# One matmul in each unit and step of the seven-product stages streams 16 to 128 more columns

## The chip, the cores and the metric

The kernel runs on one core of a Trainium2 chip. The metric is the device time in microseconds (us); the time before is the median of three runs.

## What is computed

Causal block attention over 64 heads (8 batches of 8), 576 positions and 64 dimensions, followed by a feed-forward of 4608 tokens, 512 to 2048 to 512 wide, with a leaky ReLU between:

```python
mask = block_i >= block_j                       # blocks of 64 positions
scores = np.where(mask, scale * q @ k.T, -1e9)
attn = softmax(scores)
x = (attn @ v).transpose(0, 2, 1, 3).reshape(4608, 512)
h = x @ w_in
out = np.maximum(0.01 * h, h) @ w_out
```

## The kernel before

**Two parts.** The 4608 tokens are 18 chunks of 256 (`CH`). The first ten are computed with plain products while attention goes on: `ffn1` (L909, matmuls of 256 columns at L921) and `ffn2` (L940, matmuls of 512 columns at L948). The last eight chunks are the tail. It multiplies 2 by 2 blocks with seven products in place of eight, and it is these two seven-product stages that the change touches. Every operand is kept as a high and a low part, so that one product of 256 by 256 blocks is six matmuls: for each of two 128-row halves high by high and high by low, and low by high.

**First stage, `first8`.** It runs over `k` (four pairs of token chunks) and `u` (eight units): 32 units of seven products of six matmuls (L1160), all of 256 columns. Product `j` writes the first 256 columns of a bank of PSUM; five banks of the eight are taken in turn by each unit, and the second half of such a bank is not used. The stationary operand is a weight block or a sum of weight blocks (`stationary`), the moving one a block or sum of tokens (`operand`): `new` for `j` 0 to 2. VectorE adds the products together (`sum_of`, L1173), ScalarE applies the leaky ReLU (L1176), and DMAs store the result in DRAM (`gd`, L1205).

**Second stage, `second8`.** 32 steps `n`. Step `n` loads the token side back from `gd` (L1248), forms four sums (`op2`, L970 on VectorE and L971 on GpSimd), splits everything into high and low parts (a cast, L310 on ScalarE, then a subtraction at L970: the tiles `big` and `new`), and runs seven products of six matmuls (L1288), again of 256 columns. Steps are ordered by `k`, `s` and `q`; for `q` 0 to 3 the products add up in four banks. Three of these hold two products; the fourth (`spots[4 * s + 3]`) holds product 2 in its first half and nothing in its second. After `q` 3 VectorE combines the banks (L1311) and two DMAs store them (L1324).

**The order of the instructions.** Everything is handed as operations with choices of engine, estimated costs, a rank and dependencies to `Plan.add`. `Plan.run` (L151) plays these against estimated durations: at each moment an engine that is free takes the ready operation of lowest rank, and an operation that several engines could do goes to the one that is free first. The instructions are then issued in the order so found, each engine working through its own in order. The estimate for a matmul is `RATE` (0.4462 ns) for each column, that is 114.2 ns for 256 columns; `multiply` (L189) puts matmuls one behind the other with it. A changed estimate can therefore change which engine does what, and in which order, from that moment of the plan on; whatever the plan decided before that moment stays.

Of the kernel before, what the change touches and what calls it, by code (L numbers as in the profile page):

```python
# [17 lines left out]
P = 128  # L18
# [6 lines left out]
CH = 256  # L25
# [35 lines left out]
BY1 = None  # L61
RT8 = -1.36
RM = -38.787
PACE8 = 7
GATE8 = 5
RF8 = 8.016
# [28 lines left out]
RATE = 0.4462  # L95
# [17 lines left out]
class Plan:  # L113
# [19 lines left out]
    def add(self, choices, rank, reads=(), writes=(), lag=None, kind=None):  # L133
        i = len(self.ops)
        deps = set()
        for k in reads:
            if k in self.writer:
                deps.add(self.writer[k])
        for k in writes:
            if k in self.writer:  # L140
                deps.add(self.writer[k])
            deps.update(self.readers.get(k, ()))
        for k in reads:
            self.readers.setdefault(k, []).append(i)
        for k in writes:
            self.writer[k] = i
            self.readers[k] = []
        deps.discard(i)
        self.ops.append((choices, rank, deps, lag, kind))
# [127 lines left out]
def dve2(n):  # L277
    return n / 0.96 + 110
# [15 lines left out]
def attention_ffn(ctx: ExitStack, tc: tile.TileContext, q2: bass.AP, k2: bass.AP, qk: bass.AP, v: bass.AP, w_in: bass.AP, w_out: bass.AP, out: bass.AP):  # L294
    nc = tc.nc
# [10 lines left out]
    add = plan.add  # L306
# [35 lines left out]
    later = {}  # L342
# [47 lines left out]
    wide = ExitStack()  # L390
# [466 lines left out]
    def bank(b):  # L857
        if b == 0 and SPREAD:
            banks[1] += 1
            x = banks[1] % 4  # L860
            return x, (("t", x) if x < 2 else ("o", x - 2)), (p_t + p_o)[x]
        banks[0] += 1
        x = banks[0] % 2
        return x, ("t", x), p_t[x]
# [139 lines left out]
    def tail():  # L1004
        flat = lambda ap: ap.rearrange("p a b -> p (a b)")
        spots = [(("one", y), lambda y=y: later["single"][y]) for y in range(4)]
# [12 lines left out]
        new = x8s + [(key, u, y) for key in "ST" for u in range(NU) for y in range(2)]  # L1019
# [20 lines left out]
        def sum8(u, low, name="sum8"):  # L1040
            return later[name][u][:, low].rearrange("p a b -> p (a b)")
# [75 lines left out]
        def stationary(j, u, low, d):  # L1117
            if j in (0, 4):
                return sides(u, low)[:, d + (2 if j else 0)]
            if j in (2, 5):  # L1120
                return sides(u + NU, low)[:, d + (2 if j == 5 else 0)]
            return sum8(u, low)[:, ({1: 0, 6: 1, 3: 2}[j] * 2 + d) * P :][:, :P]
# [19 lines left out]
        def first8(k, u, rank):  # L1142
            five = [(count["bank"] + y) % 8 for y in range(5)]
            count["bank"] += 5
            halves = pairs[8 * k + u]
            uses = {0: 0, 1: 1, 2: 2, 3: 3, 4: 0, 5: 4, 6: 3}
            w0, w1, ws = wkeys[("wi", u)], wkeys[("wi", u + NU)], [("S", u, 0), ("S", u, 1)]
            weights = [w0, ws, w1, ws, w0, w1, ws]
            heap = lambda h, s: heaps[halves[h]]().rearrange("p (t s c) -> p t s c", t=2, s=2)[:, :, s]
            hk = [[hkey(halves[h])] for h in range(2)]  # L1150
            if k == 0 and u < 2:
                hk = [x + [["g"], ["ob"], [], [], []][halves[h]] for h, x in enumerate(hk)]

            def product(j):
                key, bank = spots[five[uses[j]]]
                terms = [(d, w, 0) for d in range(2) for w in range(2)] + [(d, 0, 1) for d in range(2)]

                def go(n):
                    d, w, x = terms[n]
                    nc.tensor.matmul(  # L1160
                        bank()[:, :CH], stationary(j, u, w, d), operand(j, x)[:, d],
                        start=j not in (4, 6) and n == 0, stop=n == 5, skip_group_check=j in (4, 6),
                    )

                add(
                    [("PE", [(RATE * CH, lambda n=n: go(n)) for n in range(6)])], rank + j / 10,
                    [("X", j, 0), ("X", j, 1)] + weights[j], [key],
                )
                return key, lambda: bank()[:, :CH].rearrange("p (t c) -> p t c", t=2)

            def sum_of(dst, one, two, plus, reads, writes, j):
                name = "tensor_add" if plus else "tensor_sub"
                add([("DVE", dve2(CH), lambda: getattr(nc.vector, name)(dst(), one(), two()))], rank + RG8 + j / 10, reads, writes)  # L1173

            def leaky(n, dst, src, reads, writes, j):
                add([("ACT", act(n), lambda: nc.scalar.activation(dst(), src(), AF.Prelu, alpha=0.01))], rank + RG8 + j / 10, reads, writes)  # L1176

            def store(h, src, dst, reads):
                add([("SP", ISSUE, lambda: nc.sync.dma_start(dst(), src()))], rank + RG8 + 0.8, reads, [("gd", k, u, h)], lag="gs")

            q, x = divmod(u, 2)
            k0, b0 = product(0)
            add(copying(CH, lambda: heap(0, 0), b0, sb=False)[:1], rank + RG8, [k0], hk[0])
            k1, b1 = product(1)
            sum_of(lambda: heap(0, 1), lambda: heap(0, 0), b1, True, [k1], hk[0], 1)
            k2, b2 = product(2)
            sum_of(lambda: heap(1, 0), lambda: heap(0, 1), b2, True, hk[0] + [k2], hk[1], 2)
            k3, b3 = product(3)
            sum_of(lambda: heap(1, 1), lambda: heap(1, 0), b3, True, [k3], hk[1], 3)
            product(4)  # L1190
            leaky(CH, lambda: heap(0, 0), b0, [k0], hk[0], 4)
            k5, b5 = product(5)
            sum_of(lambda: heap(1, 0), lambda: heap(1, 0), b5, False, [k5], hk[1], 5)
            leaky(2 * CH, heaps[halves[1]], heaps[halves[1]], [], hk[1], 5)
            product(6)
            sum_of(lambda: heap(0, 1), lambda: heap(0, 1), b3, True, [k3], hk[0], 6)
            leaky(CH, lambda: heap(0, 1), lambda: heap(0, 1), [], hk[0], 6)
            plan.writer["unit", 8 * k + u] = len(plan.ops) - 1

            def store(a, e, src, reads, by="SP"):  # L1200
                to = lambda: gd[k][q][:, a:e, :, x].rearrange("p b s c -> p (b s) c")
                queue = {"SP": nc.sync, "ACT": nc.scalar}[by]
                cost, late = (ISSUE, 0.8) if by == "SP" else (QUEUE, 0.6)
                add(
                    [(by, cost, lambda: queue.dma_start(to(), src().rearrange("p (x c) -> p x c", c=P)))], rank + RG8 + late,  # L1205
                    reads, [("gd", k, u, a)], lag="gs",
                )

            store(2, 4, heaps[halves[1]], hk[1])
            store(0, 2, heaps[halves[0]], hk[0], "ACT")  # L1210
# [11 lines left out]
        def second8(n, rank):  # L1222
            k, s, q = (0, n % 2, n // 2) if n < 8 else (n // 8, n // 4 % 2, n % 4)
            y, us = n % 2, (2 * q, 2 * q + 1)
# [46 lines left out]
            def operand(j, low):  # L1271
                part = 0 if j in groups[0] else 1
                return area(part, low)[:, groups[part].index(j) * CH :][:, :CH], part
# [7 lines left out]
            def product(j):  # L1281
                key, to = at(j)
                terms = [(x, 0, w) for x in range(2) for w in range(2)] + [(x, 1, 0) for x in range(2)]
                part = 0 if j in groups[0] else 1

                def go(m):
                    x, low, w = terms[m]
                    nc.tensor.matmul(  # L1288
                        to(), operand(j, low)[0][:, x * P : (x + 1) * P], moving(j, us[x], w),
                        start=q == 0 and m == 0 and j in opens, stop=q == 3 and m == 5 and (spot[j][1] == 1 or j == 2),  # L1290
                    )

                reads = [("Y", part, 0, y), ("Y", part, 1, y)]
                for u in us:
                    reads += wkeys[("wo", u)] if j in (0, 3) else wkeys[("wo", u + NU)] if j in (4, 6) else [("T", u, 0), ("T", u, 1)]
                add([("PE", [(RATE * CH, lambda m=m: go(m)) for m in range(6)])], rank + order.index(j) / 10, reads, [key])

            order = (4, 5, 6, 0, 1, 2, 3) if q == 0 else (0, 4, 1, 3, 2, 5, 6) if q == 3 else range(7)
            opens = [next(j for j in order if spot[j][0] == y) for y in range(4)]
# [13 lines left out]
            key, src = at(0)  # L1313
# [47 lines left out]
    order = sorted(range(NP), key=lambda c: begin[c])  # L1361
# [4 lines left out]
    for i in range(NH + 1):  # L1366
        if i == H:
            add([("POOL", 1, narrow)], 0, [], [("h", y) for y in range(2)])
        if i == PLAIN:
            new = [(key, y) for key in ("qh", "ql", "kh", "kl") for y in range(2)]  # L1370
            add([("POOL", 1, second_stage)], 0, [y for k in wkeys.values() for y in k], new)
            new = [x for y in range(TURNS) for x in turned_keys(y) + [("back", y, c) for c in range(6)]]
# [7 lines left out]
        for c in starts.get(i, ()):  # L1380
            for u in range(NU):
                rank = begin[c] + rate[c] * u / NU
# [43 lines left out]
```

## Time and profile before

| | |
|---|---|
| runs before | 1025.39, 1032.65, 1034.58 us (median 1032.65) |
| profiled execution | 1032.74 us, its span 1031.0 us |
| TensorE matmul busy | 1005.4 us of the span, 7432 matmuls |
| first seven-product stage | about 708.8 to 865 us of the span |
| second seven-product stage | about 865 to 1026.8 us |

Times in the rows are counted from the start of the span. A matmul's recorded duration includes a modelled end that overlaps the next one, so what a matmul costs in a row of many is read from the distance between starts.

### The profile page before, as it was taken

How to read it: one execution, taken by the hardware profiler on the slowest of the kernel's cores; microseconds unless marked ns; L12 is line 12 of the kernel's file. 1: busy time of each engine (PE TensorE's matmuls, PEld its weight loads, DVE VectorE, ACT ScalarE, POOL GpSimd, SP SyncE). 2: the span in 40 equal slices, each digit the busy share in tenths (PEclk: the TensorE clock that was granted, in tenths of full speed). 3: DMA queues.
4: the chain of work that ended last, by engine and by line, in shares of the span. 5: the costliest groups of instructions: out<-in, count | busy, mean ns of one | idle time of the engine just before them, and what ended most of it. 6: DMA issues, size and time to landing. Idle time of an engine off the chain costs nothing. (4 is left out here: it accounts for less than half of the span.)

```text
span 1031.0 us, 21866 instructions
## 1 busy us (share of the span) xinstructions
PE 1005.4 (98%) x7432; PEld 899.3 (87%) x7432; DVE 783.4 (76%) x1967; ACT 638.2 (62%) x1509; POOL 425.2 (41%) x418
## 2 busy tenths in 40 slices
PE   7889999999999999999999999999999999999998
PEld 4657889888888888888888888889999999999998
DVE  6898977777978788788887778707666676877775
ACT  6788768677767667777667677636445454434332
POOL 3334437554555445454665465512131141143331
PEclk9999999999999999999999999999999999999999
DMA  6545534686777777777787687664654658455442
GB/s 208 170 153 183 157 106 148 215 245 208 212 247 224 238 226 234 226 227 243 233 245 220 207 234 219 205 196 153 195 158 130 195 171 248 149 181 179 153 158 83
DMA packets 143103, 200.52 MB, mean 194 GB/s; under 512 B 15504, under 2 KB 113552, under 8 KB 142992
## 3 DMA queue, kind: packets, MB, share of 16 engines
q1 hardware_dynamic: 126096, 190.73, 59.8%
q10 hardware_dynamic: 16896, 8.39, 2.7%
q8 instruction: 59, 0.97, 0.4%
q14 instruction: 52, 0.43, 0.1%
HBM read 117.11 MB, written 81.95 MB: 193 GB/s over the span
## 5 line engine op out<-in xcount | busy, mean ns | idle before, releaser
L921 PE MATMUL p_h<-big,wih 128*128 128x256 f32 x1024 | 203.1, 279 | 0.4 <-ACT big L310 0.4
L948 PE MATMUL p_o<-woh,big 128*128 128x512 f32 x640 | 191.5, 394 | 0.7 <-ACT piles L310 0.7
L921 PEld LDWEIGHTS p_h<-big,wih 128*128 128x128 f32 x1024 | 165.2, 188 | 5.7 <-issue 1.0
L821 DVE STREAM_TRANSPOSE turn<-prow 128x128 f32<-128x128 f32 (+3 forms) x400 | 141.9, 396 | 10.2 <-ACT prow L658 5.2
L325 POOL TENSOR_TENSOR ks<-qk_in,ks 64x576 fp32r<-64x576 f32 x83 | 122.5, 1476 | 55.1 <-DVE p_v L610 27.2
L948 PEld LDWEIGHTS p_o<-woh,big 128*128 128x128 f32 x640 | 113.3, 188 | 20.8 <-issue 1.3
L325 POOL TENSOR_TENSOR big<-piles,big 128x512 fp32r<-128x512 f32 x64 | 85.8, 1340 | 107.3 <-ACT big L310 83.3
L921 PE MATMUL p_h<-big,wil 128*128 128x256 f32 x384 | 104.4, 277 | 0.0
L948 PE MATMUL p_o<-wol,big 128*128 128x512 f32 x320 | 99.5, 392 | 0.0
L626 ACT ACTIVATE prow<-p_s,nmrec 128x448 f32<-128x448 f32 (+4 forms) x150 | 83.0, 560 | 11.3 <-DVE nmrec L617 9.5
L656 POOL TENSOR_SCALAR prow<-prow,nmrec 128x192 f32<-128x192 f32 (+4 forms) x94 | 61.0, 655 | 69.9 <-DVE nmrec L643 36.3
L658 ACT ACTIVATE prow<-prow,nmrec 128x320 f32<-128x320 f32 (+4 forms) x154 | 81.8, 566 | 4.2 <-DVE nmrec L643 3.7
L736 PE MATMUL p_v<-turn,vt 128*64 128x256 f32 (+3 forms) x700 | 76.5, 367 | 1.6 <-ACT prow L626 1.4
L626 ACT ACTIVATE prow<-p_v,nmrec 128x576 f32<-128x576 f32 (+1 forms) x150 | 71.2, 483 | 10.2 <-DVE nmrec L617 9.4
L736 PEld LDWEIGHTS p_v<-turn,vt 128*64 128x64 f32 x700 | 47.0, 137 | 29.5 <-issue 15.2
L617 DVE TENSOR_REDUCE nmrec<-p_s 128x1 f32<-128x448 f32 (+4 forms) x150 | 71.8, 514 | 0.9
L921 PEld LDWEIGHTS p_h<-big,wil 128*128 128x128 f32 x384 | 72.1, 188 | 0.2
L948 PEld LDWEIGHTS p_o<-wol,big 128*128 128x128 f32 x320 | 60.1, 188 | 13.1
L936 ACT ACTIVATE piles<-p_h 128x512 f32<-128x512 f32 x80 | 47.4, 593 | 37.2 <-PE p_h L921 34.5
L921 PE MATMUL p_h<-xh,wih 128*128 128x256 f32 x256 | 69.7, 278 | 0.0
L921 PE MATMUL p_h<-xh,wil 128*128 128x256 f32 x256 | 69.7, 278 | 0.0
L971 POOL TENSOR_TENSOR x<-x 128x256 f32<-128x256 f32 x34 | 30.5, 901 | 76.3 <-DMA x<-gd 39.0
(244 smaller groups left out, 2576.4 us busy)
## 6 DMA issues: line engine op xcount, KB each, us to landing
way<-turn SPq DMA_DIRECT2D x50, 448.0 KB, 3.4
way<-turn SPq DMA_DIRECT2D x100, 168.0 KB, 3.4
turn<-way SPq DMA_DIRECT2D x100, 168.0 KB, 3.2
qk_in<-in_qk SPq DMA_DIRECT2D x50, 288.0 KB, 3.7
turn<-way SPq DMA_DIRECT2D x100, 112.0 KB, 3.0
out<-piles SPq DMA_DIRECT2D x36, 256.0 KB, 2.4
raw<-in_w_in SPq DMA_DIRECT2D x16, 512.0 KB, 3.8
raw<-in_w_out SPq DMA_DIRECT2D x16, 512.0 KB, 3.7
```

The source lines that it names most:

```text
L325: ("POOL", pool2(n), lambda: nc.gpsimd.tensor_sub(dst(), one(), two())),
L617: [("DVE", dve(kw[t]), lambda t=t, ap=ap, flat=flat: nc.vector.tensor_reduce(nm[z][: qn[t], at_col[t] : at_col[t] + 1], ap[: qn[t]], axis= ...
L626: nc.scalar.activation(o, ap[: qn[t]], AF.Exp, bias=nm[z][: qn[t], at_col[t] : at_col[t] + 1], scale=1.0, accum_out=sums[z][: qn[t], at_co ...
L656: ("POOL", pool1(kw[t]), lambda: nc.gpsimd.tensor_scalar(p(), p(), by, 1.0, op0=ALU.mult, op1=ALU.mult)),
L658: ("ACT", act(kw[t], True) + 108, lambda: nc.scalar.mul(p(), p(), by)),
L736: nc.tensor.matmul(dst, later["vt"][z][:, j], src, start=start, stop=stop)
L821: nc.vector.transpose(dst, src.rearrange("p (s b i) -> p s b i", b=4, i=32))
L921: nc.tensor.matmul(p_h[z][:, i, :], w[:, d, f * P : (f + 1) * P], (xl if x else xh[y])[:, d, :], start=first and k == 0 and (u > 0 or i == ...
L936: add([("ACT", act(512), lambda: nc.scalar.activation(g, p_h[z], AF.Prelu, alpha=0.01))], rank, [("h", z)], ["g"])
L948: nc.tensor.matmul(p_o[m], a[:, i, m * P : (m + 1) * P], w[:, u + NU * i, :], start=u == 0 and k == 0, stop=u == NU - 1 and k == 5,)
L971: ("POOL", pool2(n), lambda: getattr(nc.gpsimd, name)(dst(), one(), two())),
```

## The change

In each unit of `first8`, the first of the six matmuls of product 1 streams `CH + more` columns in place of `CH`, from the same stationary operand; `more` is 16, 32, 64 or 128 by `u % 4`. In each step of `second8` the same is done to the first of the six matmuls of product 2, with `more` by `k % 4`, where `k` is 0 for steps 0 to 7 and `n // 8` after that. The results of the extra columns land behind the 256 columns of the product, in a part of the bank that nothing reads. The estimate that the plan is given for these matmuls grows with the columns.

```diff
+MORE = [16, 32, 64, 128]
...
                 def go(n):
                     d, w, x = terms[n]
+                    if n == 0 and j == 1:
+                        wide = later["new"][:, 1].rearrange("p d c -> p (d c)")[:, : CH + more]
+                        nc.tensor.matmul(bank()[:, : CH + more], stationary(j, u, w, d), wide, start=True, stop=False)
+                        return
...
+                more = MORE[u % len(MORE)]
                 add(
-                    [("PE", [(RATE * CH, lambda n=n: go(n)) for n in range(6)])], rank + j / 10,
+                    [("PE", [(RATE * (CH + (more if n == 0 and j == 1 else 0)), lambda n=n: go(n)) for n in range(6)])], rank + j / 10,
...
                 def go(m):
                     x, low, w = terms[m]
+                    if m == 0 and j == 2:
+                        key, bank = spots[4 * s + 3]
+                        wide = sum8(us[0], 0, "tum8")[:, : CH + more]
+                        nc.tensor.matmul(bank()[:, : CH + more], operand(j, 0)[0][:, :P], wide, start=q == 0, stop=False)
+                        return
...
-                add([("PE", [(RATE * CH, lambda m=m: go(m)) for m in range(6)])], rank + order.index(j) / 10, reads, [key])
+                more = MORE[k % len(MORE)]
+                add([("PE", [(RATE * (CH + (more if m == 0 and j == 2 else 0)), lambda m=m: go(m)) for m in range(6)])], rank + order.index(j) / 10, reads, [key])
```

## Rows read from the trace of the kernel before

**Rows 1.** The page's busy times (share of the span) of each engine.

```profile
PE 1005.4 (98%) x7432; PEld 899.3 (87%) x7432; DVE 783.4 (76%) x1967; ACT 638.2 (62%) x1509; POOL 425.2 (41%) x418
```

**Rows 2.** Busy time by stage: us, busy of each engine, granted TensorE clock, DMA.

```profile
core 0: us, PE busy (x) PEld busy (x) DVE busy (x) ACT busy (x) POOL busy (x), PEclk, DMA share, GB/s
...
708.00:865.00 157.00, 156.58 (x1360) 155.33 (x1359) 106.66 (x237) 77.47 (x173) 35.73 (x33) 1.00 0.56 169
865.00:889.00 24.00, 21.72 (x176) 20.81 (x177) 17.62 (x26) 10.37 (x13) 4.37 (x5) 1.00 0.58 182
889.00:1027.00 138.00, 137.78 (x1170) 137.57 (x1169) 102.01 (x168) 51.48 (x62) 44.06 (x47) 1.00 0.46 151
```

**Rows 3.** Waits of PE, 708 to 1031 us: us in total, times, longest.

```profile
PE p_x L1288 <- DVE big L970: 1.7, 3, 0.8
PE p_h L1288 <- DVE big L970: 0.5, 1, 0.5
PE p_h L1160 <- ACT more L310: 0.3, 1, 0.3
PE p_x L1160 <- DVE xin L1173: 0.2, 1, 0.2
```

**Rows 4.** Chain that ended last, in order of time: start us, us, what.

```profile
860.92 1.36 PE p_h L1160 x12
...
866.69 6.39 DMA x<-gd
...
873.24 0.75 POOL x L971
...
874.92 1.06 ACT big L310
...
876.01 1.50 DVE big L970
...
881.99 3.92 DMA xin<-gd
...
887.19 1.23 DVE big L970
888.42 0.04 issue
888.47 4.75 PE p_x L1288 x38
...
908.06 19.79 PE p_x L1288 x168
...
1024.66 2.13 PE p_o L1288 x18
```

**Rows 5.** PE in order of time: start us, us, instruction, count; 512 columns, then 256.

```profile
703.26 0.62 PE L948 MATMUL p_o<-woh,big 128*128 128x512 f32 x2
...
708.76 0.28 PE L1160 MATMUL p_x<-new,wih 128*128 128x256 f32 x1
...
715.61 0.28 PE L1160 MATMUL p_x<-new,wih 128*128 128x256 f32 x1
...
721.73 0.28 PE L1160 MATMUL p_h<-new,wih 128*128 128x256 f32 x1
```

**Rows 6.** PE in order of time, attention's scores of 448 and 320 columns.

```profile
600.37 1.03 PE L596 MATMUL p_v<-ks,qs 128*128 128x288 f32 x7
601.23 0.86 PE L596 MATMUL p_s<-ks,qs 128*128 128x448 f32 x4
601.93 0.63 PE L948 MATMUL p_o<-woh,big 128*128 128x512 f32 x2
```

**Rows 7.** Groups by shape, 708 to 1031 us: busy us, mean ns, idle before.

```profile
L970 DVE TENSOR_TENSOR big<-xin,big 128x1024 fp32r<-128x1024 f32 x16 | 21.1, 1318 | 8.2 <-ACT big L310 8.1
L971 POOL TENSOR_TENSOR sum<-sum 128x768 fp32r<-128x768 f32 x4 | 7.9, 1976 | 26.1 <-ACT sum L310 26.1
```

## The prediction

> **What bounds the kernel now.** I read the busy times first, then the busy times by stage, then what TensorE waits for, and last the chain that ended last, each answering what the one before left open. TensorE has matmuls on record for 1005.4 of 1031.0 us, far ahead of VectorE's 783.4 [rows 1]. By stage: in the first seven-product stage it is busy for 156.58 of 157 us, around the change to the second for 21.72 of 24, and from 889 to 1027 for 137.78 of 138 [rows 2]. So in the stretch that the change touches TensorE has no room to take in more work. What it waits for there adds up to 1.7 + 0.5 + 0.3 + 0.2 = 2.7 us [rows 3]; 2.2 of them are waits for the low parts of `big` (L970 on VectorE) at the start of the second stage. The chain says the same: from 888.47 us to the end of the last product it is TensorE and nothing else (888.47 to 1024.66 + 2.13 = 1026.79), and ahead of that it runs for some 22 us through loads from `gd`, GpSimd, ScalarE and VectorE [rows 4]. The reader should see two regimes: 157 us and 138 us where a nanosecond added to TensorE is a nanosecond added to the end, and 24 us between them where the way through DRAM counts as well.
>
> **The change, part by part.**
>
> *The columns.* In `first8` each of the four values of `more` falls to 2 units in each of 4 pairs, 8 units in all: 8 x (16 + 32 + 64 + 128) = 1920 columns. In `second8` steps 0 to 7 have 16, and the next three eights 32, 64 and 128: again 1920. That is 3840 columns in 64 matmuls; no matmul, weight load, DMA, or instruction on another engine is added, and none is taken away.
>
> *The price of a column.* No row shows a matmul of 272 to 384 columns inside these stages, so I take it from distances between starts. The 24 matmuls of 512 columns from 703.26 to 708.76 us take 5.50 / 24 = 229.2 ns each; the 54 of 256 columns from 715.61 to 721.73 take 6.12 / 54 = 113.3 ns each [rows 5]. The slope between them is (229.2 - 113.3) / 256 = 0.453 ns for a column. In the second stage 168 matmuls of 256 columns take 19.79 us, 117.8 ns each [rows 4], or 0.460 for a column if it is proportional. A test between the two widths: the four score matmuls of attention (two of 448 and two of 320 columns, 1536 in all) take 601.93 - 601.23 = 0.70 us, 0.456 for a column [rows 6]. So 1920 x 0.453 + 1920 x 0.460 = 0.87 + 0.88 = 1.75 us.
>
> Could some of it be free, because a matmul of 256 columns is held at 113 ns by something else, such as the weight load beside it? The group before gives a hint of such a floor: seven matmuls (four of 288, two of 192, one of 128 columns) take 601.23 - 600.37 = 0.86 us [rows 6]; take 4 x 288 x 0.453 = 0.52 for the wide ones, and the three narrow ones have 0.34 left, 113 ns each, though they have fewer columns than 256. But 512 columns cost 229.2 / 113.3 = 2.02 times what 256 cost, so from 256 on nothing is left to hide in, and I take the slope in full. The bounds: nothing at all (the floor were above 256 columns; the 2.02 speaks against it), and 0.86 / 1664 = 0.517 ns for a column, the dearest row, which makes 1.98 us.
>
> The Trainium skill prices this too (TensorE: Matmul & The Clock Gate, Back-to-back issue gap). It gives an isolated gap of columns / 2.4 GHz + 2.5 ns, by which the extra would be 3840 / 2.4 = 1.60 us; the trace agrees in kind, with a slope of 0.453 where the page has 0.417. The same section gives about 81 ns for 128 and 131 ns for 512 columns when a stream of loads and matmuls is sustained, which would make a column 0.13 ns and the whole change 0.5 us; the 229.2 ns at 512 columns are against that. None of the terms below uses these figures.
>
> *PSUM and the waits.* The extra results lie in the half of a bank that holds nothing else, and the extra operand columns belong to tiles that one cast wrote together with the first 256, so no new wait for an operand arises. Costed at nothing; no reader of that half exists that could be late.
>
> *The plan.* The larger estimates (7 to 57 ns a unit or step) move the plan's clock of TensorE. Up to the first wide matmul (about 709 us) the order is the old one. After that, ties between engines can fall differently: an addition may go to GpSimd in place of VectorE or trade places with its neighbour. This is the one part whose cost no row gives. From below: all 2.7 us of TensorE's waits vanish. From above: an operand comes late. The stages bear much: between 889 and 1027 us VectorE is busy for 102.01 of 138 us, ScalarE for 51.48 and GpSimd for 44.06 [rows 2]. The order was also made for 114.2 ns a matmul (0.4462 x 256) and is run at 117.8: 42 x 3.6 = 151 ns adrift in every step, more than the 57 ns that the widest matmul adds, and TensorE waits for nothing there. So I take zero, and say what is late if that is wrong: in the 24 us between the stages the low part of `big` (L970, 1318 ns [rows 7]) gets its turn on VectorE behind another operation, TensorE waits on its first product, and all later products queue behind it. An operation that gets in the way costs up to its length: 1.3 us on VectorE, up to 1.98 on GpSimd [rows 7]. The first steps of the second stage, 16 columns (7 ns) each, can hide in the waits there; that is under 0.1 us.
>
> *The sum.* 1032.74 of the profiled execution + 1.75 + 0 = 1034.5 us. The profiled execution lies 0.1 us above the median of the runs shown, so the median is forecast at 1034.5 too.
>
> **The rivals.**
>
> *A new wait makes it slower.* The plan's new order puts work ahead of the loads or splits between 865 and 889 us. For it: that stretch already has 2.2 us of waits, and its chain has two loads from `gd` of 6.39 and 3.92 us with GpSimd, ScalarE and VectorE in turn behind them [rows 4]; a store or load issued one place later shifts all of it. Against it: ranks don't change, and the steps before the first wait have work ready. Price: one load's time again, 6.4 us, plus one operation of 1.98: 1034.5 + 8.4 = 1042.9. It decides (over 1% slower) from 10.3 - 1.75 = 8.6 us of new waits on.
>
> *The pace of the matmuls shifts.* At 877.9 us the distance between starts goes from 113.3 to 117.8 ns and stays there [rows 4, 5], with the granted clock at 1.00 in the rows of both stretches [rows 2]. No row says why. The runs shown differ by 9.2 us, and such stretches can be a cause. If the second stage kept 113.3, its 149 us would be 149 x 4.5 / 117.8 = 5.7 us shorter: 1028.8. If the first stage (169 us from 708.8 to 877.9) ran at 117.8, it would be 169 x 4.5 / 113.3 = 6.7 us longer: 1041.2.
>
> *The columns are free, or the new order is a better one.* Free columns give 1032.7; columns paid and all of the 2.7 us of waits gone give 1031.8. For over 1% faster some 12 us would have to go, and the waits and the pace together hold 8.4.
>
> **How the numbers follow.** The forecast as worked out: 0.62. Pace faster 0.10, slower 0.10. New waits 0.13, of which 0.08 go past the 8.6 us. Free columns or fewer waits 0.05. The likeliest is 1034.5. The range goes from the fast pace with the waits gone (1028.8 - 2.7, about 1026) to the slow pace of the first stage (1041); what is left out on top is the 0.08 of many waits and a part of the slow pace, below some 0.05. About 1% is what a measurement of this kernel can tell from no change. Over 1% faster: 0.03, only by causes that I don't see in the rows. Over 1% slower: 0.09, the new waits and a run that adds them to the slow pace. Within 1%: 0.88.
>
> **What would show it right or wrong.** The profile after should have as many matmuls (7432) and distances from the start of a wide matmul to the next of about 120, 128, 142 and 171 ns for 272, 288, 320 and 384 columns in the first stage. TensorE's waits from 708 us on should stay under some 4 us, and the stage to 889 and the one after it be longer by about 0.9 us each, when the pace is the same. Free columns would show as 113 ns for 272 columns and 0.5 us or less in all. A new wait would show as TensorE waiting on `big` or `new` (L970, L310) for over 5 us, or on sums of the first stage (L1173). If the waits and the pace stay and the time still moves by more than 3 us, the price of a column is wrong, and with it the prediction.

## The result, and the profile after

The changed kernel takes 1036.2 us (median of 20 runs, 1034.37 to 1038.71) against 1032.31 us of the kernel before (20 runs, 1025.39 to 1038.87). The ratio is 1.0054, 95% interval 1.0036 to 1.0072: 3.7 to 7.4 us slower, 5.6 in the middle. That is within 1%, as forecast, and within the range, but the 1.75 us forecast is below the interval.

The profiled execution took 1035.08 us with a span of 1033.3 us. The busy times of the engines (share of the span, instructions):

```profile
PE 1007.6 (98%) x7432; PEld 902.4 (87%) x7432; DVE 786.9 (76%) x1970; ACT 637.7 (62%) x1509; POOL 430.2 (42%) x415
```

The same 7432 matmuls; but VectorE has three operations more than in [rows 1] and GpSimd three fewer: the plan has dealt some work out differently. TensorE's own order changed too. Step 0 of the second stage used to begin with three products from `big`, followed by the three from `new`; after the change the three from `new` come first. The first matmuls of step 0 before the change:

```profile
865.05 0.74 PE L1288 MATMUL p_x<-sum,big 128*128 128x256 f32 x4
```

and after it:

```profile
869.58 0.28 PE L1299 MATMUL p_x<-woh,new 128*128 128x256 f32 x1
```

Busy times by stage (us, busy of each engine, granted clock, DMA):

```profile
708.00:865.00 157.00, 156.95 (x1336) 155.78 (x1335) 106.67 (x236) 75.89 (x169) 34.38 (x29) 1.00 0.55 164
...
865.00:892.00 27.00, 23.57 (x187) 22.97 (x187) 18.18 (x29) 12.16 (x17) 8.42 (x6) 0.94 0.63 192
892.00:1027.00 135.00, 135.00 (x1171) 135.00 (x1169) 102.86 (x165) 51.30 (x62) 44.84 (x47) 1.00 0.48 155
```

Either side of the change of stage TensorE is as full as in [rows 2]. Between 865 and 892 us it is idle for 3.4 us, and the granted clock is 0.94 where [rows 2] has 1.00. TensorE's waits from 708 us on (us in total, times, longest):

```profile
PE p_h L1299 <- ACT big L311: 1.6, 1, 1.6
PE p_o L1165 <- DVE piles L1179: 1.3, 1, 1.3
PE p_h L1299 <- DVE big L971: 0.5, 1, 0.5
```

3.4 us in three waits, where [rows 3] has 2.7 in six. TensorE in order of time, with the idle time before in brackets, shows what follows them:

```profile
868.77 0.96 PE L1165 MATMUL p_o<-big,sum 128*128 128x256 f32 x6 [1.30 <-DVE piles L1179]
...
876.14 0.74 PE L1299 MATMUL p_h<-sum,big 128*128 128x256 f32 x4 [1.60 <-ACT big L311]
877.39 0.50 PE L1299 MATMUL p_h<-sum,big 128*128 128x256 f32 x2 [0.52 <-DVE big L971]
877.73 0.29 PE L1297 MATMUL p_o<-sum,big 128*128 128x272 f32 x1
877.86 0.94 PE L1299 MATMUL p_o<-sum,big 128*128 128x256 f32 x5
878.59 0.42 PE L1299 MATMUL p_h<-woh,big 128*128 128x256 f32 x1
878.81 0.42 PE L1299 MATMUL p_h<-wol,big 128*128 128x256 f32 x1
879.03 0.41 PE L1299 MATMUL p_h<-woh,big 128*128 128x256 f32 x1
```

From 878.3 us the distance between starts is 0.21 to 0.22 us for 256 columns in place of 0.113: TensorE runs at 1.2 GHz, the lower of its two levels, right behind the waits of 1.60 and 0.52 us, and is back at 2.4 GHz 3.4 us later. The Trainium skill says that this clock follows how busy TensorE has been (TensorE: Matmul & The Clock Gate, What's actually happening); this row agrees in kind, and the runs below show that not every such wait brings it.

Why TensorE had to wait is read from VectorE in order of time:

```profile
864.31 0.41 DVE L1179 TENSOR_TENSOR xin<-xin,p_x 128x256 f32<-128x256 f32 x1
866.93 0.42 DVE L971 TENSOR_TENSOR x<-x 128x256 f32<-128x256 f32 x1 [2.21 <-DMA x<-gd]
867.27 0.92 DVE L1179 TENSOR_TENSOR piles<-piles,p_h 128x256 f32<-128x256 f32 x2
868.30 0.42 DVE L1179 TENSOR_TENSOR piles<-piles,p_o 128x256 f32<-128x256 f32 x1
```

and from GpSimd in the trace of the kernel before:

```profile
863.27 0.74 POOL L971 TENSOR_TENSOR x<-x 128x256 f32<-128x256 f32 x1 [3.18 <-DMA x<-gd]
```

The last token-side subtraction of step 0 waits for a load from `gd`. Before, GpSimd did it and stood still for 3.18 us, with nothing behind it that was needed. In the new order VectorE has it, stands still for 2.21 us, and the product sums of the last unit queue behind it. Product 6 of that unit, on TensorE, waits for the third of them (868.30, L1179) before it may add to its bank. The chain that ended last goes on from there to the second wait (start us, us, what; short pieces of issue time are left out):

```profile
868.77 0.75 PE p_o L1165 x4
869.52 0.41 DVE piles L1179
...
869.95 0.95 ACT piles L1182 x2
...
870.92 2.42 DMA gd<-piles
...
873.35 0.75 POOL xin L972
...
874.47 0.43 DVE xin L971
...
875.04 1.05 ACT big L311
...
876.12 1.24 DVE big L971
```

Late sums, a late store to DRAM, a late load of step 1, a late `big`, and TensorE's 1.60 us.

The wide matmuls cost what their columns cost. In the same chain, farther on, each wide matmul is a piece of its own, up to the start of the next (288, 320 and 384 columns):

```profile
918.63 0.13 PE p_x L1297
...
957.27 0.15 PE p_x L1297
...
1001.53 0.17 PE p_x L1297
```

**A ledger of the tail.** For every trace I took each distance between the starts of two matmuls that follow each other, from the first matmul of the first stage to the last of the second. 113.34 ns (the mean of the distances at the faster pace) for 256 columns, 229 ns for each of the twelve matmuls of `ffn2` among them, is the base, 307.3 us for all (310.4 with the matmuls added in `after_filled`). The extra columns are counted at 113.34 / 256 = 0.443 ns. What is left of a distance is put down to the half clock if it lies in such a stretch, to waits if over 0.1 us, and to the slower pace (117.8 ns) otherwise. All in us; "start" is when the first matmul of the tail starts:

| kernel | start | tail | columns | slower pace | half clock | waits |
|---|---|---|---|---|---|---|
| before | 708.76 | 317.74 | 0 | 5.75 | 0 | 4.73 |
| after | 709.18 | 319.64 | 1.70 | 4.34 | 1.51 | 4.83 |
| columns_only | 709.94 | 319.03 | 1.70 | 4.29 | 0 | 5.77 |
| order_only | 708.74 | 320.32 | 0 | 5.25 | 1.60 | 6.21 |
| columns_256 | 709.01 | 324.54 | 7.25 | 6.70 | 0 | 3.32 |
| after_filled | 708.35 | 319.60 | 1.70 | 4.73 | 0 | 2.73 |
| same_again | 706.17 | 319.14 | 0 | 6.15 | 1.50 | 4.22 |
| first256 | 706.96 | 323.85 | 3.63 | 8.98 | 0 | 3.97 |
| second256 | 707.76 | 317.82 | 3.63 | 4.37 | 0 | 2.56 |
| grid_neither | 708.61 | 316.72 | 0 | 5.38 | 0 | 4.08 |
| grid_columns | 710.86 | 317.31 | 1.70 | 4.22 | 0 | 4.12 |
| grid_order | 708.09 | 319.35 | 0 | 4.51 | 0 | 7.58 |
| grid_both | 710.71 | 321.31 | 1.70 | 5.39 | 1.31 | 5.64 |
| one_op | 706.92 | 320.14 | 1.70 | 4.40 | 1.50 | 5.27 |

Between the two profiled executions the tail grew by 1.90 us: columns 1.70, half clock 1.51, waits 0.10, and the slower pace gave 1.41 back. Each row is one execution, and the rows of equal kernels show how far two executions lie apart.

**The wider matmuls set the pace of those behind them.** The column "slower pace" hides two large terms of opposite sign. In the first stage, rows of the changed kernel around a matmul of 320 and one of 384 columns:

```profile
721.67 0.30 PE L1163 MATMUL p_x<-new,sum 128*128 128x320 f32 x1
...
723.11 0.87 PE L1165 MATMUL p_x<-big,sum 128*128 128x256 f32 x6
723.81 0.87 PE L1165 MATMUL p_h<-big,sum 128*128 128x256 f32 x6
...
726.64 0.34 PE L1163 MATMUL p_x<-new,sum 128*128 128x384 f32 x1
...
730.12 0.84 PE L1165 MATMUL p_x<-big,sum 128*128 128x256 f32 x6
```

Behind the first, six matmuls of 256 columns are recorded with 0.87 us (0.70 us from start to start, 117 ns each), behind the second with 0.84. In all six traces with 16 to 128 columns more, the matmuls behind every 320-column one of the first stage, up to the next wide one 41 or 47 of them, stand about 117.8 ns apart; behind every 384-column one it is about 114 until the change of stage begins. Over the first 132 us of the tail, 36% of the distances are at the slower pace in each of these six, which costs 1.85 us; with matmuls of 512 columns, behind most of which the pace changes over, forth and back, it is some 50% and 2.43 us. In the six traces without a wider matmul in the first stage it is 0.02 us. So the first stage loses as much again as its and the second stage's columns cost together.

The second stage gains. From 186 us after the start of the tail, every distance is at the slower pace in the old order without wider matmuls there (4.9 to 5.2 us in four traces), and 3.9 to 4.3 us remain in the new one; with 16 to 128 columns more it is 1.6 us in five traces and 2.4 in `grid_both`, with 512 columns 3.0 and 3.2. In the changed kernel's chain, 47 matmuls behind a 320-column one and behind a 384-column one:

```profile
951.74 5.54 PE p_x L1299 x47
...
991.38 5.33 PE p_x L1299 x47
```

Why the width of one matmul does this to the dozens behind it, no run shows.

### The profile page after: what moved, and what is told of

The parts are those of the page before. It is cut to its first block, busy times and chain, and to the rows that moved or that the text cites. A ratio compares the mean times of both kernels' runs of the same rounds, so it can differ in the third digit from the quotient of the medians.

```text
span 1033.3 us, 21864 instructions
## 1 busy us (share of the span) xinstructions
PE 1007.6 (98%) x7432; PEld 902.4 (87%) x7432; DVE 786.9 (76%) x1970; ACT 637.7 (62%) x1509; POOL 430.2 (42%) x415
## 5 line engine op out<-in xcount | busy, mean ns | idle before, releaser
L737 PE MATMUL p_v<-turn,vt 128*64 128x192 f32 (+3 forms) x700 | 76.6, 367 | 0.2 <-ACT prow L627 0.2
L972 POOL TENSOR_TENSOR x<-x 128x256 f32<-128x256 f32 x30 | 27.9, 932 | 81.0 <-DVE x L971 48.5
```

The source lines that it names most:

```text
L737: nc.tensor.matmul(dst, later["vt"][z][:, j], src, start=start, stop=stop)
L972: ("POOL", pool2(n), lambda: getattr(nc.gpsimd, name)(dst(), one(), two())),
```

## The experiments

Each ratio is to the kernel before, on the same chip; 1% is 10.3 us.

**columns_only: wider matmuls, old order.** At both places in the changed kernel:

```diff
-RATE * (CH + (more if n == 0 and j == 1 else 0))
+RATE * CH
...
-RATE * (CH + (more if m == 0 and j == 2 else 0))
+RATE * CH
```

> The wide matmuls of the change, but the plan is given the old estimate (RATE x 256) for them, so that every engine has the order of the kernel before. Theory (the columns cost 0.45 ns each, the rest of the change's 5.6 us comes from the new order): +1.75 us, ratio 1.0017, waits of TensorE from 708 us on as before (2.7 us), granted clock 1.00 throughout. Rival (the columns themselves cost about three times the forecast): +5.6 us, ratio 1.0054, with starts behind a 384-column matmul far more than 171 ns away.

Ratio 1.0042 (1.0027 to 1.0058): 4.3 us, between theory and rival. The trace is with the theory on the price: the wide matmuls' distances are 122, 128, 144 and 174 ns in the mean (16 of each), the columns add up to 1.70 us, and there is no stretch at half clock. TensorE's waits are 3.6 us in place of the 2.7 expected. What the other 2.6 us of the ratio are this one execution doesn't show.

**order_only: new order, all matmuls at 256 columns.**

```diff
-if n == 0 and j == 1:
+if False:
...
-if m == 0 and j == 2:
+if False:
```

> All matmuls have 256 columns again, but the plan is given the larger estimates, so that every engine has the order of the changed kernel. Theory (the new order brings waits of 1.3, 1.6 and 0.5 us between 867 and 878 us and behind them some 3.5 us at half the granted clock): +3 to +4 us, ratio 1.003 to 1.004, and the same dip of the clock in the profile. Rival (the columns are the cost): 0 us, ratio 1.000.

Ratio 1.0033 (1.0013 to 1.0054): 3.4 us with no column added, as the theory has it. TensorE's waits from 700 us on:

```profile
PE p_o L1165 <- DVE piles L1179: 1.9, 1, 1.9
PE p_h L1299 <- DVE big L971: 1.0, 2, 0.5
PE p_x L1299 <- DVE big L971: 0.8, 1, 0.8
PE p_h L1299 <- ACT big L311: 0.4, 1, 0.4
```

4.1 us, the wait of product 6 for the product sums first. The clock falls here too, from 866.7 us, behind the 1.9 us wait (1.60 us in the ledger).

**columns_256: 64 matmuls of 512 columns, old order.**

```diff
-MORE = [16, 32, 64, 128]
+MORE = [256, 256, 256, 256]
```

together with the edit of `columns_only`.

> Order of the kernel before, but each of the 64 wide matmuls streams 256 more columns (512 in all): 64 x 256 = 16384 columns. Theory (0.453 to 0.460 ns for a column, nothing hidden): +7.5 us, ratio 1.0072. Rival (a floor hides the first columns, or a sustained stream is paid at 0.13 ns for a column): +2 us, ratio 1.002. Rival (three times the forecast): +23 us, ratio 1.022.

Ratio 1.0111 (1.0084 to 1.0139): 11.4 us, over the 7.5 forecast. The 64 wide matmuls stand 230 ns before the next in the mean, the 229.2 of [rows 5]. From `columns_only` to here it is 7.1 us for 16384 - 3840 = 12544 columns, 0.57 ns each, with intervals of 1.6 and 2.8 us to either side on the two ends: the slope doesn't contradict 0.45, and the rivals of 0.13 ns and of three times the price are out.

**after_filled: the changed kernel with TensorE's three waits filled.**

```diff
+        def busy(count):
+            for _ in range(count):
+                nc.tensor.matmul(p_o[1][:, CH:], wih[:, 0, :P], wih[:, 1, :CH], start=False, stop=False, skip_group_check=True)
...
                     d, w, x = terms[n]
+                    if (k, u, j, n) == (3, 7, 6, 0):
+                        busy(11)
...
                     x, low, w = terms[m]
+                    if n == 1 and j == 1 and m in (0, 4):
+                        busy(4 if m else 13)
```

> The changed kernel in its own order, with 28 matmuls of 256 columns put into TensorE's three waits between the stages (11 ahead of product 6 of the last unit, 13 and 4 in product 1 of step 1); they read weights that are long in place and write columns that nothing reads. They fill 28 x 113 = 3.2 us of the waits' 3.4 and add no work to the result. Theory (the idle time makes the granted clock fall to half for some 3.5 us): the clock stays at 1.00 between 865 and 891 us and the time falls by about 1.7 us against the changed kernel, ratio to the kernel before about 1.0035. Rival (the fall of the clock has another cause, or costs nothing): ratio 1.0054, or more where the filling delays the products.

```profile
865.00:892.00 27.00, 26.67 (x223) 25.94 (x222) 19.75 (x30) 11.71 (x15) 5.71 (x6) 1.00 0.58 175
...
PE p_o L1171 <- DVE piles L1185: 0.2, 1, 0.2
```

(The busy times of the stage change, and a wait of TensorE.) The clock stays at 1.00 and the wait of product 6 is down to 0.2 us, but the kernel is no faster: 1.0071 (1.0036 to 1.0106, seven runs). The ledger says why: the filling itself is 3.2 us, and it saves 2.1 of waits and 1.5 of half clock. That the clock stayed up fits with idle time as what lets it fall; by itself one execution shows no more, since some executions of the unfilled kernels stay up too.

**same_again: nothing changed.** The wide branches off and the old estimates, which is the kernel before under other line numbers.

> The text of the changed kernel with both wide branches switched off and the old estimates: instruction for instruction the kernel before, under other line numbers. It shows what the comparison gives for no change and, with its profile, how much waits and pace vary between executions of one order. Theory (the 2.5 us by which the columns alone came out dearer than their distances between starts are real): ratio 1.000 within 0.0015. Rival (they are a matter of how kernels are compared): ratio about 1.0025.

Ratio 1.0014 (0.9990 to 1.0039). The comparison of equal kernels can be off by 1.4 us, then; this neither clears nor takes away the 2.6 us. The trace held a surprise. TensorE in order of time:

```profile
885.75 0.59 PE L1299 MATMUL p_x<-woh,big 128*128 128x256 f32 x2 [2.31 <-DVE big L971]
886.13 2.13 PE L1299 MATMUL p_x<-sum,big 128*128 128x256 f32 x9
```

Nine matmuls in 2.13 us: half clock, behind a wait of 2.31 us. The old order has the fall as well, in some executions. It isn't a property of the new order alone.

**first256 and second256: 256 columns more, in one stage only, old order.** `columns_256` with the other stage's branch set to `if False:`.

> Old order; only the 32 wide matmuls of the first stage, each with 256 more columns (8192 in all). Theory A (what comes on top of the 0.453 ns a column lies in TensorE's waits between the stages, since a first stage that ends later, or the pace there, moves them): +3.7 us for the columns and some 2 us more, ratio 1.0055. Theory B (it lies in the second stage): +3.7 us, ratio 1.0036.

> Old order; only the 32 wide matmuls of the second stage, each with 256 more columns (8192 in all). Theory A (the excess lies between the stages or in the first): +3.8 us, less what the waits there hide, ratio 1.0035. Theory B (it lies in the second stage): +5.8 us, ratio 1.0056.

Ratios 1.0081 (1.0052 to 1.0110) and 1.0038 (1.0010 to 1.0066): 8.3 and 3.9 us for columns of 3.63 us each. The second stage's columns cost their price; what comes on top goes with the first stage (theory A), by 1.7 to 7.7 us, but not in the way I expected: the waits are no longer (3.97 us in the ledger). What differs is the pace. In `first256` some 1940 distances of the tail are at the slower one, against some 1260 in the kernel before: the wide matmuls bring it into the first stage (2.43 us there, against 0.02), and the second stage stays slow as it was. In `second256` the first stage is at the faster pace and the wide matmuls take 2 us of slower pace out of the second. Between the two traces that makes 4.6 us (8.98 and 4.37), as much as the two ratios lie apart (4.4).

**The grid: neither, columns, order, both, on one chip.** The edits are those of `same_again`, `columns_only` and `order_only`; `grid_both` is the changed kernel.

> First of four on one chip: neither wider matmuls nor larger estimates, the kernel before under other line numbers. Theory (the change costs 1.7 us of columns, the rest is TensorE's waits between the stages and the stretches at half clock behind them, which come with the order, and a scatter of 1 to 2 us that a comparison of equal kernels shows too): ratio 1.000 to 1.0015. Rival (columns carry a cost that doesn't show in the distances between starts): 1.000.

> Second of four: wider matmuls in the old order. Theory: 1.7 us over the first of the four, the 2.5 us more that the first comparison gave are scatter and don't come back. Rival: again 4 us over it.

> Third of four: the new order without wider matmuls. Theory: 2 to 3.5 us over the first of the four, with a mean granted clock some 0.001 lower than its. Rival (the order costs nothing): 0 us.

> Fourth of four: the changed kernel itself. Theory: 4 to 5.5 us over the first of the four, the sum of the second and the third. Rival (the two interact, wider matmuls fill waits of the new order): less than the sum by over 1.5 us.

| kernel | ratio | interval | us | mean granted clock of its runs |
|---|---|---|---|---|
| grid_neither | 0.9998 | 0.9973 to 1.0022 | -0.2 | 0.9973 |
| grid_columns | 1.0030 | 1.0004 to 1.0056 | 3.1 | 0.9987 |
| grid_order | 1.0036 | 1.0009 to 1.0063 | 3.7 | 0.9975 |
| grid_both | 1.0082 | 1.0055 to 1.0110 | 8.4 | 0.9968 |

The order costs 3.7 us by itself, as in `order_only`. The columns again come out above their 1.7 us (3.1, interval 0.4 to 5.8). From the means of the four kernels' runs, the columns cost 3.6 us (some 2.1 to 5.0) averaged over both orders, and the order 4.7 (some 3.3 to 6.1) averaged with and without columns; so to call the excess scatter, as I did, isn't borne out. Both together are no less than the sum (6.8). The clock went against my forecast: the mean of `grid_order` isn't below that of `grid_neither`. All four profiled executions also have a fall of the clock between 48 and 78 us, in a stretch that the change doesn't touch. The waits of `grid_order`:

```profile
PE p_o L1165 <- DVE piles L1179: 1.8, 1, 1.8
PE p_h L1299 <- ACT big L311: 1.7, 1, 1.7
PE p_h L1299 <- DVE big L971: 1.0, 2, 0.5
PE p_x L1299 <- DVE big L971: 0.9, 1, 0.9
```

5.4 us, and in this execution the clock stayed at 1.00 there: a wait of 1.8 us needn't bring the fall. Of the traces with the new order and no mend, three of four have the fall at the change of stage (after, order_only, grid_both); of the eight traces of the old order, with and without wider matmuls, one (same_again).

**one_op: the one subtraction back on GpSimd.** In the changed kernel:

```diff
-op2(CH, lambda: cells(6, 7), lambda: cells(4, 5), lambda: cells(3, 4), False, rank + RS8, [near[4], near[3]], [near[6]])
+op2(CH, lambda: cells(6, 7), lambda: cells(4, 5), lambda: cells(3, 4), False, rank + RS8, [near[4], near[3]], [near[6]], "POOL" if n == 0 else None)
```

> The changed kernel with one operation tied to GpSimd: the last of the four token-side subtractions of step 0, which waits for the third load from DRAM. In the changed kernel it stands on VectorE, waits 2.2 us for that load, and three product sums queue behind it; in the kernel before it stood on GpSimd. The order differs from the changed kernel's in some twenty operations around the change of stage and nowhere else. Theory (this one operation makes TensorE's waits of 1.3 and 1.6 us and the half clock behind them): no wait of VectorE on that load, TensorE's waits between 865 and 892 us down to 1 us or less in all, granted clock 1.00 there, and some 3 us off the changed kernel's ratio, about 1.003 to 1.004. Rival (the waits come from TensorE's own order or from the loads): waits of 1.3 us or more as before the mend, ratio 1.0054 to 1.008.

TensorE's waits:

```profile
PE p_h L1299 <- ACT big L311: 1.9, 1, 1.9
PE p_x L1299 <- ACT new L311: 1.2, 1, 1.2
PE p_h L1299 <- DVE big L971: 0.5, 1, 0.5
PE p_x L1299 <- DVE new L971: 0.3, 1, 0.3
```

The link is confirmed, the theory isn't. VectorE no longer waits for that load, and the wait of product 6 for the product sums is gone from the list. But 1.2 us of waiting came back at the first split of step 0 (`new`, a cast on ScalarE), the 1.9 us at step 1 stayed, the clock fell behind it, and the ratio is 1.0078 (1.0049 to 1.0108). The subtraction was one late thing of several: taking out one wait showed the next. That in the new order the whole way through DRAM at the change of stage runs late against TensorE is how I read this; it isn't shown. Around the change of stage some eleven operations of VectorE, ScalarE and GpSimd stand in another place, and three of TensorE's own products. Which of them would have to go back isn't settled, and whether TensorE's own order is the cause was not tested.

## Why the prediction was right or wrong

**What bounds the kernel: right.** Outside the change of stage TensorE is full before and after, and added columns show up in full in the distances.

**The price of a column: right for the matmul itself.** Forecast 0.453 and 0.460 ns, 1.75 us in all. The ledger's 0.443 and 1.70 are in proportion to 256 columns; measured against the mean distance of the 256-column ones up to twelve places away, the wide matmuls of `columns_only` and `grid_columns` stand 1.72 and 1.69 us longer, 0.447 and 0.441 ns a column. The distances named for 272 to 384 columns in the first stage (120, 128, 142, 171 ns) came out at 121, 128, 142 and 178 in `columns_only`. There is no floor above 256 columns. The hint of one at narrower widths was a misreading: in that group of scores the distances of the three narrow matmuls are 90, 61 and 88 ns, and the four of 288 columns take 132 to 184. Of the Trainium skill's figures (TensorE: Matmul & The Clock Gate, Back-to-back issue gap) the isolated gap is the near one (an estimate from it for 512 columns is 215.8 ns; measured 229.2), and the sustained one of about 131 ns doesn't hold for these matmuls. The prediction's last sign, a time that moves by more than 3 us while waits and pace stay, showed in `columns_only` (4.3 us); but there the pace didn't stay, and the distances hold the price directly.

**PSUM and the waits of the wide matmuls: right as far as it goes.** No wide matmul stands in any list of TensorE's waits, and with the old order TensorE waits mostly for the low parts of `big` with the wider matmuls as without.

**The plan at zero: this step failed.** The new order costs 3.4 and 3.7 us in two comparisons without a single added column, twice the columns' price. I had the place (865 to 889 us), the mechanism (an operation gets its turn behind another, and what TensorE needs queues behind it) and the kind of swap (GpSimd against VectorE), and priced it as unlikely. That TensorE's own products could change places I had not. The reason I gave was the steady stretch, where the order bears 151 ns of drift a step without a wait. That nearly held: from 892 us on TensorE waits for nothing in the profile after, and once, for 0.8 to 0.9 us near 915 us, in `order_only`, `grid_order` and `after_filled`. But it was read off the wrong stretch. The stage change has no such room, and there [rows 3, 4] already had a chain of loads with TensorE waiting on it. Two orders there differ by 1.5 to 3.5 us of waits (4.1 to 4.7 in the three traces of the old order, 6.2 and 7.6 in the two of the new one without wider matmuls). With wider matmuls the waits don't tell the orders apart: 4.8 and 5.6 us with the new one, 2.6 to 5.8 with the old.

**What I left out: the clock.** Of the six traces in which TensorE waits for 1.6 us or longer at the change of stage, five show it at half clock for 3.4 us behind such a wait, which costs another 1.3 to 1.6 us. The rows of before had no stretch like it; the old order has it too, in other executions. So a wait at this place can be charged with some 1.5 us more than its length.

**The rivals.** The new wait came in small, 3.4 us of waits where 8.6 of new ones would have been needed for over 1%. The rival on the pace came true in part, both ways at once, and the change itself brought it: 36% of the first stage at the slower pace (1.85 us dearer), and in the second most of it at the faster (3.3 us cheaper in `columns_only` and `grid_columns`). I had taken the pace as something that comes from outside and put its term at zero. That its two halves pull against each other, to a net gain of 1.1 to 1.9 us in these traces, is luck: nothing in the sum foresaw it. Whether the pace is also what makes the runs before scatter is not shown. Free columns are out.

**Open.** The time of whole runs rises by more than the columns' price. With the old order it was 4.3 (2.8 to 6.0) and 3.1 us (0.4 to 5.8), over both orders of the grid 3.6 (2.1 to 5.0), where the matmuls themselves show 1.7; and the intervals of `columns_256` and `first256` lie above their columns' price too. Chance alone hardly covers that. The pace covers most of it in `first256`, but in `columns_only` and `grid_columns` it makes the tail shorter, so the ledger's tails explain none of the excess. In these two profiled executions the time lies ahead of the first wide matmul (tails start at 709.94 and 710.86 us, against 706.17 to 708.76 in the three traces of the old order without them), where the instructions are the same: between 98 and 708 us TensorE waits 3.3 and 2.4 us for ScalarE's `prow` in attention, against 0.5 to 1.4 in those three. But `after` and `grid_both`, with the same wider matmuls, have 0.2 and 0.5 us of these waits, so one profile each doesn't tie them to the columns. The excess of some 2 us has no shown cause.

## What to carry to other kernels

Columns that are added to a matmul on a full TensorE cost some 0.44 ns each here, and a distance between starts in the trace prices that matmul well. Look at the distances behind it as well: here the pace of dozens of matmuls changed with the width of one, in sum by more than the columns cost, and the time of whole runs rose by some 2 us more than the columns explain. In a kernel whose order is made by a planner, an edit of an estimate by some tens of ns is an edit of the order: price it at the tightest place behind it, not at the steady stretch. And when one wait there is taken out, look for the next before counting it as gained.

## What the runs showed of the hardware that I had not expected

- Two paces of the same matmul at a granted clock of 1.00: 113.3 and 117.8 ns for 256 columns, in long stretches, in every trace. The width of a single matmul ahead sets which: about 117.8 behind every 320-column one of the first stage and about 114, until the change of stage, behind every 384-column one, in six traces of six; behind most 512-column ones the pace changes over. No run here tells why.
- TensorE at half clock for 3.4 us behind waits of 1.6 us (with 0.5 more close behind), 1.9 and 2.3 us, but in `grid_order` not behind waits of 1.8 and 1.7 us, and in `grid_both` not behind one of 2.2 us, only behind the next (1.6 and 0.5).
